# Fused chunked attention and a two-layer block: program order by a list scheduler, whole-chunk attention, ordered loads, quarter stripes

## The chip, the cores and the metric

The kernel runs on one core of one Trainium2 chip. Its engines are named as in the profiles: PE or TensorE (matmuls; PEld is its weight load), ACT or ScalarE and DVE or VectorE (element-wise work and copies), POOL or GpSimd (most casts of Q and K here, and the weight loads), SP or SyncE (issues the other loads and the stores). Matmuls write to PSUM, and a copy by ACT or DVE takes the result from there. The metric is the device time of one execution in microseconds (us). Repeated executions of one kernel mostly agree within 0.5%, a few are 1% longer. A profiled execution also has a span, from its first instruction to its last; the reported time is some 1.7 us longer than the span (265.2 against 263.5 us in the profiled run of the kernel before).

## The reference

Linear attention with a decay per head, in blocks, followed by two matrix products with a smooth activation between them (4 batches, 8 heads, 768 tokens, head dimension 64; 3072 tokens, model width 512, hidden width 2048):

```python
for b in range(nb):                                # blocks of 64 tokens
    intra = einsum('bhic,bhjc->bhij', qb, kb) * Dmask
    intra = einsum('bhij,bhjd->bhid', intra, vb)
    inter = einsum('bhid,bhde->bhie', qb * lam_pow, kv_state)
    out[:, :, sl] = intra + inter
    kv_state = lam_block * kv_state + einsum('bhsd,bhse->bhde', kb_dec, vb)
x = out.transpose(0, 2, 1, 3).reshape(3072, 512)
h = x @ w_in
g = where(h >= 1, h, where(h <= -1, 0, (h + 1) ** 2 / 4))
return g @ w_out
```

## The kernel before

Both kernels fold the decay into Q and K by tables, and work on 24 chunks of 128 tokens. Four chunks make a stripe of 512 tokens. A stripe goes through the first layer (16 blocks of 128 hidden units, four 128x512 matmuls each, into `ph`), ReLU on ACT, the rest of the activation on DVE (`t`, `w`, `gT`), and the second layer (16 groups of four 128x512 matmuls into `py`). Attention works on half chunks (four heads), and each half passes through three stages with one PSUM buffer each:

```python
def stage_t(u):     # transposes of Q, K with V and identity; copies out of PSUM
    ...             # 2 transposes into pq, 2 matmuls 128x256 into pk
    for hi in range(2):
        nc.scalar.copy(out=qb[hi*64:hi*64+64, :, hi, :], in_=pq[hi*64:hi*64+64])
    nc.scalar.copy(out=t, in_=pk[:, :, 1, :])                       # kT
    nc.vector.tensor_tensor(t, pk[:, :, 0, :], U[u - 2], op=AX.add) # running state
def stage_s(u):     # scores, 2 matmuls 128x256, then the causal mask on DVE
    ...
def stage_o(u):     # state and scores times V into po, then two copies to xT on ACT
    ...
```

The order is written by hand. Before the main loop stripe 0 is attended and chunk 4 begun; in the loop a block of the first layer of stripe `s` alternates with a step of attention for stripe `s+1` and a group of the second layer of stripe `s-1`:

```python
load_w_in(...)                       # rest of the first weights
for i in range(WS):
    load_w_out(i)                    # second weights, all at once
ensure_loaded(CPS + 1)
ensure_cast(CPS)                     # chunk 4
a, b_ = att_step()
for f in a + b_:
    f()
...
for s in range(NST + 1):
    for i in range(FO):
        ...                          # loads, casts
        if s < NST:
            l1(s, i)
        for f in todo_a:             # attention of later chunks
            f()
        if s < NST:
            smelu(s, i)
        if s > 0:
            l2(s - 1, i)             # second layer: one stripe behind
        for f in todo_b:
            f()
```

So the second layer of stripe 0 stands behind the first block of stripe 1, and that needs all four chunks of stripe 1 attended.

Of the kernel before, what the change touches and what calls it, by code (L numbers as in the profile page):

```python
# [23 lines left out]
def kernel(  # L24
# [18 lines left out]
    C = 128  # L43
# [11 lines left out]
    NU = NCH * 2  # L55
# [3 lines left out]
    ld = ctx.enter_context(tc.tile_pool(name="ld", bufs=6))  # L59
    qkp = ctx.enter_context(tc.tile_pool(name="qkp", bufs=3))  # L60
    ktp = ctx.enter_context(tc.tile_pool(name="ktp", bufs=3))
    scp = ctx.enter_context(tc.tile_pool(name="scp", bufs=2))
    up = ctx.enter_context(tc.tile_pool(name="up", bufs=3))
    xp = ctx.enter_context(tc.tile_pool(name="xp", bufs=3))
    gp = ctx.enter_context(tc.tile_pool(name="gp", bufs=2))
    rp = ctx.enter_context(tc.tile_pool(name="rp", bufs=3))
# [4 lines left out]
    pp_q = ctx.enter_context(tc.tile_pool(name="pp_q", bufs=1, space=PS))  # L71
    pp_k = ctx.enter_context(tc.tile_pool(name="pp_k", bufs=1, space=PS))
# [6 lines left out]
    qkv_ld = {}  # L79

    def load(c):
        b, s0 = c // NCB, (c % NCB) * C
        ts = []
        for name, src in (("q", q), ("k", k), ("v", v)):
            t = ld.tile([128, H, D], F32, name=f"{name}f", tag=f"{name}f")
            nc.sync.dma_start(out=t, in_=src[b, :, s0:s0 + C, :].rearrange("h p d -> p h d"))
            ts.append(t)
        qkv_ld[c] = ts

    lam_b = const.tile([128, H], F32)  # L90
    nc.sync.dma_start(out=lam_b, in_=lam.partition_broadcast(128))
    load(0)
    load(1)
# [7 lines left out]
    nc.gpsimd.iota(pos_i, pattern=[[C, NCB]], base=-S // 2, channel_multiplier=1)  # L101
    pos = const.tile([128, NCB], F32)
    nc.vector.tensor_copy(pos, pos_i)
    arg = const.tile([128, NCB, H], F32)
# [5 lines left out]
    causal = const.tile([128, 128], F32)  # L110
    nc.gpsimd.memset(causal, 1.0)
    nc.gpsimd.affine_select(
        out=causal, in_=causal, compare_op=AX.is_ge, fill=0.0,
        base=0, pattern=[[1, 128]], channel_multiplier=-1)
    one = const.tile([128, 1], F32)
    nc.vector.memset(one, 1.0)

    NQ = 3
    qbd = []
    for i in range(NQ):  # L120
        t = const.tile([128, 2, 2, 128], BF16, name=f"qbd{i}")
        nc.vector.memset(t, 0.0)
        qbd.append(t)
    NV = 3
    vi = []
    for i in range(NV):
        t = const.tile([128, HP, 2, 128], BF16, name=f"vi{i}")
        nc.vector.tensor_copy(t[:, :, 1, :], _bc(ident, 1, HP))
        vi.append(t)
# [8 lines left out]
    def load_w_in(i):  # L138
        n = d_ff // WS
        nc.gpsimd.dma_start(out=w_in_sb[:, :, i * n:(i + 1) * n], in_=w_in_r[:, :, i * n:(i + 1) * n])  # L140

    def load_w_out(i):
        n = FO // WS
        nc.gpsimd.dma_start(out=w_out_sb[:, i * n:(i + 1) * n, :], in_=w_out_r[:, i * n:(i + 1) * n, :])


    qs, ks = {}, {}

    def cast(c, k_eng):
        qf, kf, vf = qkv_ld.pop(c)  # L150
        cb = c % NCB
        t = qkp.tile([128, H, D], BF16, name="qs", tag="qs")
        nc.gpsimd.tensor_tensor(t, qf, _bc(tab_q[:, cb, :], 2, D), op=AX.mult)  # L153
        qs[c] = t
        t = qkp.tile([128, H, D], BF16, name="ks", tag="ks")
        k_eng.tensor_tensor(t, kf, _bc(tab_k[:, cb, :], 2, D), op=AX.mult)  # L156
        ks[c] = t
        nc.scalar.copy(out=vi[c % NV][:, :, 0, :], in_=vf.rearrange("p (a b) d -> p a (b d)", b=2))  # L158

    kT, U, sc_sb, xT = {}, {}, {}, {}  # L160

    def stage_t(u):
        c, hf = u // 2, u % 2
        cb = c % NCB
        pq = pp_q.tile([128, 2, 128], BF16, name="pq", tag="pq")
        pk = pp_k.tile([128, 2, 2, 128], F32, name="pk", tag="pk")
        for j in range(2):
            hp = 2 * hf + j
            nc.tensor.transpose(out=pq[:, j, :], in_=qs[c][:, 2 * hp:2 * hp + 2, :].rearrange("p a d -> p (a d)"),  # L169
                                identity=ident)  # L170
        for j in range(2):
            hp = 2 * hf + j
            nc.tensor.matmul(pk[:, j], lhsT=ks[c][:, 2 * hp:2 * hp + 2, :].rearrange("p a d -> p (a d)"),  # L173
                             rhs=vi[c % NV][:, hp], start=True, stop=True)
        qb = qbd[u % NQ]
        for hi in range(2):
            nc.scalar.copy(out=qb[hi * 64:hi * 64 + 64, :, hi, :], in_=pq[hi * 64:hi * 64 + 64])  # L177
        t = ktp.tile([128, 2, 128], BF16, name="kT", tag="kT")
        nc.scalar.copy(out=t, in_=pk[:, :, 1, :])  # L179
        kT[u] = t  # L180
        if cb < NCB - 1:
            t = up.tile([128, 2, 128], BF16, name="U", tag=f"U{hf}")
            if cb == 0:
                nc.vector.tensor_copy(t, pk[:, :, 0, :])
            else:
                nc.vector.tensor_tensor(t, pk[:, :, 0, :], U[u - 2], op=AX.add)  # L186
            U[u] = t

    def stage_s(u):
        ps = pp_s.tile([128, 4, 128], F32, name="ps", tag="ps")  # L190
        for j in range(2):
            nc.tensor.matmul(ps[:, 2 * j:2 * j + 2, :], lhsT=kT[u][:, j, :], rhs=qbd[u % NQ][:, j],  # L192
                             start=True, stop=True)
        t = scp.tile([128, 4, 128], BF16, name="sc", tag="sc")
        nc.vector.tensor_tensor(t, ps, _bc(causal, 1, 4), op=AX.mult)  # L195
        sc_sb[u] = t

    def stage_o(u):
        c, hf = u // 2, u % 2
        cb = c % NCB  # L200
        st, off = c // CPS, (c % CPS) * C
        po = pp_o.tile([128, 2, 2, 128], F32, name="po", tag="po")
        for j in range(2):
            hp = 2 * hf + j
            if cb > 0:
                nc.tensor.matmul(po[:, j], lhsT=U[u - 2][:, j, :], rhs=qbd[u % NQ][:, j], start=True, stop=False)  # L206
            nc.tensor.matmul(po[:, j], lhsT=vi[c % NV][:, hp, 0, :], rhs=sc_sb[u][:, 2 * j:2 * j + 2, :],  # L207
                             start=(cb == 0), stop=True)
        if st not in xT:
            xT[st] = xp.tile([128, KO, MS], BF16, name="xT", tag="xT")  # L210
        for hi in range(2):
            nc.scalar.copy(out=xT[st][hi * 64:hi * 64 + 64, 2 * hf:2 * hf + 2, off:off + C],  # L212
                           in_=po[hi * 64:hi * 64 + 64, :, hi, :])

    def att(i):

        u, odd = i // 2, i % 2
        a, b_ = [], []
        if not odd:
            if u < NU:  # L220
                a.append(lambda: stage_t(u))
            if 1 <= u <= NU:
                b_.append(lambda: stage_o(u - 1))
        elif u < NU:
            a.append(lambda: stage_s(u))
        return a, b_


    gT, r_t, py_t = {}, {}, {}

    def l1(s, ni):
        ph = pp_h.tile([128, MS], F32, name="ph", tag="ph")
        for ko in range(KO):
            nc.tensor.matmul(ph, lhsT=w_in_sb[:, ko, ni * 128:(ni + 1) * 128], rhs=xT[s][:, ko, :],  # L234
                             start=(ko == 0), stop=(ko == KO - 1))
        if ni % 2 == 0:
            r_t[s] = rp.tile([128, 2, MS], BF16, name="r", tag="r")
        nc.scalar.activation(out=r_t[s][:, ni % 2, :], in_=ph, func=AF.Relu, bias=one[:, 0:1])  # L238

    def smelu(s, ni):  # L240
        if ni % 2 == 0:
            return
        r = r_t[s]
        if ni == 1:
            gT[s] = gp.tile([128, FO, MS], BF16, name="gT", tag="gT")
        t = rp.tile([128, 2, MS], BF16, name="t1", tag="t1")
        nc.vector.tensor_scalar(t, r, 0.5, 1.0, op0=AX.mult, op1=AX.min)
        w = rp.tile([128, 2, MS], BF16, name="w1", tag="w1")
        nc.vector.tensor_tensor(w, r, t, op=AX.subtract)  # L249
        nc.vector.tensor_tensor(gT[s][:, ni - 1:ni + 1, :], w, t, op=AX.mult)  # L250

    def l2(s, i):
        ms, kg = i // 4, i % 4
        if kg == 0:
            py_t[s] = pp_y.tile([128, d_model], F32, name="py", tag="py")
        py = py_t[s]
        for ko in range(4 * kg, 4 * kg + 4):
            nc.tensor.matmul(py, lhsT=gT[s][:, ko, ms * 128:(ms + 1) * 128], rhs=w_out_sb[:, ko, :],  # L258
                             start=(ko == 0), stop=(ko == FO - 1))
        if kg == 3:  # L260
            o = op.tile([128, d_model], F32, name="osb", tag="osb")
            nc.scalar.copy(out=o, in_=py)  # L262
            m0 = s * MS + ms * 128
# [40 lines left out]
    for f in a + b_:  # L304
        f()
# [60 lines left out]
```

## Time and profile before

263.2 us (median; 263.1 to 264.8).

| Stretch of the span, us | TensorE busy | what is there |
|---|---|---|
| 0 to 30 | 15.3 of 30 | attention of stripe 0 |
| 30 to 40 | 0 | nothing |
| 40 to 80 | 29.0 of 40 | first layer of stripe 0, attention of stripe 1 |
| 80 to 200 | 119.3 of 120 | everything interleaved, TensorE full |

From the page of the kernel before, its second part: one digit for each fortieth of the span (6.6 us), the busy share in tenths; `PEclk` is the recorded clock of TensorE in tenths, `DMA` the busy share of the DMA engines, `GB/s` what they moved.

```profile
PE   0567306666889999999999999999999999999993
ACT  4768303778996977797779777977796754554210
PEclk9999755999999999999999999999999999999998
DMA  6999999999990526753574357110111011111122
GB/s 134 210 217 187 196 196 220 210 226 218 218 202 2 138 67 120 159 128 85 108 159 121 88 113 163 40 40 0 42 41 40 2 40 40 40 42 40 40 80 80
```

The first twelve slices (to 78 us) have the DMA full and TensorE half idle; from then on it is the other way round. The table of windows of the same kernel gives busy us of each engine in each stretch, the number of its instructions, the recorded clock, the DMA share and GB/s.

```profile
core 0: us, PE busy (x) PEld busy (x) DVE busy (x) ACT busy (x) POOL busy (x), PEclk, DMA share, GB/s
30.00:40.00 10.00, 0.00 (x0) 0.10 (x1) 0.00 (x0) 0.00 (x0) 1.04 (x1) 0.65 1.21 196
40.00:50.00 10.00, 6.85 (x27) 3.29 (x27) 1.12 (x2) 4.90 (x11) 2.69 (x3) 0.67 1.16 213
50.00:60.00 10.00, 6.89 (x43) 3.96 (x45) 8.74 (x11) 8.12 (x20) 5.83 (x6) 1.00 1.14 225
60.00:70.00 10.00, 6.78 (x45) 3.72 (x45) 8.36 (x15) 8.68 (x23) 2.59 (x2) 1.00 1.32 218
70.00:80.00 10.00, 8.50 (x53) 4.84 (x53) 8.92 (x15) 9.56 (x23) 4.64 (x4) 1.00 1.16 189
80.00:100.00 20.00, 19.89 (x118) 11.10 (x119) 12.64 (x24) 15.48 (x36) 4.08 (x4) 1.00 0.30 74
```

The waits from 20 to 80 us name the longest one (us in total, times, longest):

```profile
PE pk L173 <- ACT vi_152 L158: 12.6, 1, 12.6
ACT vi_152 L158 <- DMA vf<-in_v_dram: 11.9, 1, 11.9
```

and TensorE's timeline (start, duration, instruction, what ended the idle time before it) shows the hole it makes:

```profile
28.55 0.42 PE L169 MATMUL pq<-ident,qs 128*128 128x128 bf16 x2
41.53 0.58 PE L173 MATMUL pk<-vi_152,ks 128*128 128x256 bf16 x2 [12.56 <-ACT vi_152 L158]
```

TensorE takes its instructions in order. Chunk 4's matmuls wait for V; chunk 3's last step and the first layer of stripe 0, whose weights had landed by 31.2 us, stand behind them.

The same timeline gives the price of matmuls, from start to start. At full rate ("warm" below), two of 128 columns take 0.11 us, two of 256 take 0.22, four of 512 take 0.86 (the last from four blocks in a row elsewhere); early in the run one of 256 columns takes 0.21 to 0.22 us, half the rate:

```profile
19.68 0.42 PE L206 MATMUL po<-qbd_144,U 128*128 128x256 bf16 x1
19.90 0.42 PE L207 MATMUL po<-sc,vi_152 128*128 128x256 bf16 x1
...
120.33 0.28 PE L169 MATMUL pq<-ident,qs 128*128 128x128 bf16 x2
120.44 0.38 PE L173 MATMUL pk<-vi_152,ks 128*128 128x256 bf16 x2
120.66 1.03 PE L258 MATMUL py<-w_out_sb,gT 128*128 128x512 bf16 x4
```

### The profile page before, as it was taken

Reading aid. Unit: us, or ns where it says so; the run is one execution under the profiler, and the core shown is the slowest. Engines: PE = TensorE matmul, PEld = TensorE weight load, DVE = VectorE, ACT = ScalarE, POOL = GpSimd, SP = SyncE. Lnnn points to the kernel's source line nnn. Section 1 sums busy time; section 2 is a strip of 40 time slices with the busy share of each in tenths; the row PEclk is TensorE's granted clock in tenths of the full one; section 3 lists DMA queues with packets and bytes.
Section 4 is the critical chain, followed back from the end, with each engine's and each line's share of the span. In section 5 each row is a group of like instructions: output and inputs, shape, how many; then the busy total and the mean of one; then the engine's idle time right before and its main releaser. Section 6 shows DMA issues by size and latency. Waiting matters only on the chain.

```text
span 263.5 us, 3576 instructions
## 1 busy us (share of the span) xinstructions
PE 222.8 (85%) x1209; PEld 118.7 (45%) x1232; DVE 143.8 (55%) x245; ACT 173.7 (66%) x389; POOL 54.2 (21%) x61
## 2 busy tenths in 40 slices
PE   0567306666889999999999999999999999999993
PEld 0234203333445555555555555555555544444441
DVE  3554201388887576657574766574747645555300
ACT  4768303778996977797779777977796754554210
POOL 3418111552340332033303320333000000000000
PEclk9999755999999999999999999999999999999998
DMA  6999999999990526753574357110111011111122
GB/s 134 210 217 187 196 196 220 210 226 218 218 202 2 138 67 120 159 128 85 108 159 121 88 113 163 40 40 0 42 41 40 2 40 40 40 42 40 40 80 80
DMA packets 82721, 29.58 MB, mean 112 GB/s; under 512 B 75536, under 2 KB 79632, under 8 KB 82704
## 3 DMA queue, kind: packets, MB, share of 16 engines
q1 hardware_dynamic: 78480, 25.18, 45.5%
q0 software_dynamic: 4224, 4.19, 9.7%
q8 instruction: 9, 0.15, 0.3%
q14 instruction: 8, 0.07, 0.1%
HBM read 27.27 MB, written 6.29 MB: 127 GB/s over the span
## 4 chain that ended last, share of the span: by engine, by line
PE 69%; DVE 3%; ACT 1%; issue 0%; ACTq 0%
PE py L258 31%; PE ph L234 26%; PE po L207 3%; PE ps L192 3%; PE pk L173 2%; PE po L206 2%; PE pq L169 1%; DVE gT L250 1%; DVE w_726 L249 1%; DVE sc L195 0%; DVE w_768 L249 0%; ACT r L238 0%; DVE U L186 0%; ACT xT L212 0%; ACT osb L262 0%
## 5 line engine op out<-in xcount | busy, mean ns | idle before, releaser
L234 PE MATMUL ph<-xT,w_in_sb 128*128 128x512 bf16 x380 | 99.6, 383 | 1.7 <-ACT r L238 1.3
L238 ACT ACTIVATE r<-ph,one 128x512 bf16<-128x512 f32 x96 | 65.9, 687 | 43.3 <-PE ph L234 39.6
L258 PE MATMUL py<-w_out_sb,gT 128*128 128x512 bf16 x365 | 92.3, 379 | 1.0
L234 PEld LDWEIGHTS <-w_in_sb 128*128 128x128 bf16 x384 | 37.9, 99 | 37.6 <-issue 2.8
L258 PEld LDWEIGHTS <-gT 128*128 128x128 bf16 x384 | 37.6, 98 | 32.3
L153 POOL TENSOR_TENSOR qs<-qf,tab_q 128x512 bf16<-128x512 f32 x24 | 25.3, 1052 | 121.7 <-PE pq L169 92.0
L186 DVE TENSOR_TENSOR U<-pk,U 128x256 bf16<-128x256 f32 x32 | 13.6, 424 | 56.5 <-ACT kT L179 56.5
L212 ACT CAST xT<-po 64x256 bf16<-64x256 f32 x96 | 35.3, 367 | 4.5 <-PE po L207 3.7
L195 DVE TENSOR_TENSOR sc<-ps,causal 128x512 bf16<-128x512 f32 x48 | 32.9, 685 | 4.6 <-PE ps L192 4.0
L156 POOL TENSOR_TENSOR ks<-kf,tab_k 128x512 bf16<-128x512 f32 x20 | 22.3, 1117 | 7.9 <-DMA kf<-in_k_dram 7.9
L262 ACT COPY osb<-py 128x512 f32<-128x512 f32 x24 | 14.2, 591 | 12.4 <-PE py L258 12.4
L169 PE MATMUL pq<-ident,qs 128*128 128x128 bf16 x96 | 14.3, 235 | 6.7 <-POOL qs L153 6.7
L179 ACT CAST kT<-pk 128x256 bf16<-128x256 f32 x48 | 17.9, 372 | 2.4 <-PE pk L173 1.3
L173 PE MATMUL pk<-vi_152,ks 128*128 128x256 bf16 x32 | 6.8, 298 | 14.6 <-ACT vi_152 L158 12.6
L169 PEld LDWEIGHTS <-qs 128*128 128x128 bf16 x96 | 10.1, 106 | 16.8 <-POOL qs L153 6.7
L173 PEld LDWEIGHTS <-ks 128*128 128x128 bf16 x96 | 8.1, 103 | 20.5 <-issue 8.1
L192 PEld LDWEIGHTS <-kT 128*128 128x128 bf16 x96 | 8.5, 101 | 19.4 <-ACT kT L179 11.0
L158 ACT CAST vi_152<-vf 128x512 bf16<-128x512 f32 x8 | 4.9, 610 | 11.9 <-DMA vf<-in_v_dram 11.9
L177 ACT COPY qbd_146<-pq 64x256 bf16<-64x256 bf16 x32 | 11.6, 361 | 1.6 <-PE pq L169 1.2
L177 ACT COPY qbd_144<-pq 64x256 bf16<-64x256 bf16 x32 | 11.5, 361 | 0.6 <-PE pq L169 0.2
L177 ACT COPY qbd_148<-pq 64x256 bf16<-64x256 bf16 x32 | 11.5, 361 | 0.5
L206 PEld LDWEIGHTS <-U 128*128 128x128 bf16 x80 | 8.2, 102 | 7.8 <-issue 3.7
(187 smaller groups left out, 213.9 us busy)
## 6 DMA issues: line engine op xcount, KB each, us to landing
qf<-in_q_dram SPq DMA_DIRECT2D x24, 256.0 KB, 4.8
kf<-in_k_dram SPq DMA_DIRECT2D x24, 256.0 KB, 4.7
vf<-in_v_dram SPq DMA_DIRECT2D x24, 256.0 KB, 5.0
out_dram<-osb SPq DMA_DIRECT2D x24, 256.0 KB, 2.0
w_in_sb<-in_moe_w_in_dram POOLq DMA_DIRECT2D x4, 512.0 KB, 8.7
w_out_sb<-in_moe_w_out_dram POOLq DMA_DIRECT2D x4, 512.0 KB, 15.5
lam_b<-in_lam_dram SPq DMA_DIRECT2D x1, 4.0 KB, 2.9
```

What stands on the lines that cost most here:

```text
L153: nc.gpsimd.tensor_tensor(t, qf, _bc(tab_q[:, cb, :], 2, D), op=AX.mult)
L156: k_eng.tensor_tensor(t, kf, _bc(tab_k[:, cb, :], 2, D), op=AX.mult)
L169: nc.tensor.transpose(out=pq[:, j, :], in_=qs[c][:, 2 * hp:2 * hp + 2, :].rearrange("p a d -> p (a d)"), identity=ident)
L173: nc.tensor.matmul(pk[:, j], lhsT=ks[c][:, 2 * hp:2 * hp + 2, :].rearrange("p a d -> p (a d)"), rhs=vi[c % NV][:, hp], start=True, stop=True)
L177: nc.scalar.copy(out=qb[hi * 64:hi * 64 + 64, :, hi, :], in_=pq[hi * 64:hi * 64 + 64])
L179: nc.scalar.copy(out=t, in_=pk[:, :, 1, :])
L192: nc.tensor.matmul(ps[:, 2 * j:2 * j + 2, :], lhsT=kT[u][:, j, :], rhs=qbd[u % NQ][:, j], start=True, stop=True)
L195: nc.vector.tensor_tensor(t, ps, _bc(causal, 1, 4), op=AX.mult)
L212: nc.scalar.copy(out=xT[st][hi * 64:hi * 64 + 64, 2 * hf:2 * hf + 2, off:off + C], in_=po[hi * 64:hi * 64 + 64, :, hi, :])
L234: nc.tensor.matmul(ph, lhsT=w_in_sb[:, ko, ni * 128:(ni + 1) * 128], rhs=xT[s][:, ko, :], start=(ko == 0), stop=(ko == KO - 1))
L238: nc.scalar.activation(out=r_t[s][:, ni % 2, :], in_=ph, func=AF.Relu, bias=one[:, 0:1])
L258: nc.tensor.matmul(py, lhsT=gT[s][:, ko, ms * 128:(ms + 1) * 128], rhs=w_out_sb[:, ko, :], start=(ko == 0), stop=(ko == FO - 1))
```

## The change

Its intent is to have TensorE full from as early as possible. Four parts:

1. Every operation (load, cast, group of matmuls, copy) becomes a node with an engine, an estimated duration, the nodes that it needs (buffers that come free included) and a deadline. A list scheduler plays the graph through on estimated durations and emits the program in that order.
2. Attention works on whole chunks: all eight transposes at once, copies twice as wide, the running state kept in PSUM by accumulation instead of DVE additions, all matmuls 128 columns wide. ACT loses most of its copies; DVE takes over those of K, and those of Q from chunk 4 on.
3. Loads are ordered: K, Q, V of chunks 0 to 3, first weights, chunk 4, second weights, the rest.
4. Stripes 1 and 2 go through the first layer in quarters of 128 tokens, so that one attended chunk gives TensorE 16 blocks' worth of work, and the second layer of that quarter follows. The second layer of stripe 0 no longer waits for stripe 1.

The core of the diff (cuts marked):

```diff
+    def run_plan(free):
+        ...                                  # deadlines go backwards through the graph
+        while len(out_seq) < len(ops):
+            t, e = min((max(free[e], min(r for r, _ in lst)), e) for e, lst in ready.items() if lst)
+            r, x = min(((r, x) for r, x in ready[e] if r <= t), key=lambda p: (p[1].due, p[0]))
+            ready[e].remove((r, x))
+            free[e] = t + x.ns
+            x.t, x.end = t, t + x.ns + x.extra
+            out_seq.append((t, len(out_seq), x))
+            ...
+        for t, _, x in sorted(out_seq, key=lambda p: p[:2]):
+            x.fn()                           # emits the instructions
...
+    QS = (1, 2)
+    ...
+        if s in QS:
+            l1 = [(1, s, i, p) for p in range(CPS) for i in range(0, FO, CPS)]
+        else:
+            l1 = [(1, s, i, 0) for i in range(FO)]
...
+    order = [("c", c) for c in range(CPS)] + [("w", 0), ("c", CPS), ("w", 1)] + [("c", c) for c in range(CPS + 1, NCH)]
...
+        add(("t", c), "PE", mm(*[128] * 8), lambda c=c: f_t(c),
+            [("cast", c, 0), ("cast", c, 1), ("kb", c - 1, 0), ("kb", c - 1, 1), ("qT", c - 1)], due=od - 6000, extra=FILL)
+        add(("qT", c), e, 600 if c < CPS else 365, ...)
+        add(("x", c), "ACT", 600, lambda c=c: f_x(c), ...)
...
+            add(("g", grp), "DVE", 220 + 512 * rw * 1.25 / .96 + 240, lambda a=(s, i, n, p, grp): f_g(*a),
+                [("r", n1), ("g", grp - 1), ("l2", (s - 1) * FO - 1)])
...
-    for s in range(NST + 1):
-        for i in range(FO):
-            ...                              # the order by hand
+    run_plan({"PE": 7000, "ACT": 6500, "DVE": 6000, "POOL": 7000, "DMA": 2000})
```

## The prediction

> **What bounds the kernel now.** From 78 us on, TensorE: the table of windows has PE 99.4% busy from 80 to 240 us, and the timeline shows matmuls back to back until 259.46 us; then 4 us of last eviction and store. Before 78 us TensorE waits: PE is busy 15 of the first 30 us, 0 of 30 to 40, 13.7 of 40 to 60, 15.3 of 60 to 80. The waits view: 12.6 us (28.6 to 41.5) behind the V cast of chunk 4, whose load came late behind weights; waits on copies of K; ACT 90% busy from 60 to 80. Matmuls ran at half rate (256 columns every 0.21 us instead of 0.11) from 6.7 to 22.8 us and from 26 to 46.6. The slices show DMA near 210 GB/s up to 78 us.
>
> **What the change does.** Warm spacing in the timeline is 0.216 us for 512 columns, 0.110 for 256, 0.055 for 128. TensorE before: 768 x 0.216 + 368 x 0.110 + 96 x 0.055 = 211 us. After, by the program text: attention 736 matmuls of 128 columns (40.9 us against 45.8), the first layer of stripes 1 and 2 as 512 of 128 columns instead of 128 of 512, four groups split 384+128: 208 us. So only 3 us of work goes. ACT loses query copies (34.6 us), K copies (17.9) and half-width xT copies (35.3 to some 14), and gains U copies: 174 to about 120 us. DVE stays near 145.
>
> The gain is the head. K, Q, V of chunks 0 to 3 load first, then first weights, chunk 4, second weights, the rest. 256 KB takes about 1.22 us at 215 GB/s, a weight quarter about 3 us (9.7% of 263 us over 8). So chunk 3 is in at 18 us, stripe 0 attended at 23, first weights complete near 30, second near 46, chunk 5 near 50. Between 23 and 46 us TensorE has 13.9 us of first layer, 1.7 of attention, 3.6 of chunk 4's quarter, 5 of second layer: just enough. Afterwards a chunk costs 3.7 us of DMA against 8.6 of TensorE.
>
> **Sum.** Dense start 23 + (207.7 - 6.3 done by then) + 2.5 for half-rate matmuls at first (before: 5 us at half rate from 41.5) + 3 for gaps up to 50 us + 4 tail = **234 us, range 229 to 243**. Chances: faster by over 2% 0.96, within 2% 0.03, slower 0.01. The saving, 29 us, is all on the critical path: the dense part begins 55 us earlier but must do most of what the old head had done.
>
> **What would show it.** Windows: PE nearly full from 25 us, over 98% after 50; the chain almost all PE. 128-column spacing 55 ns. No V-cast wait over 3 us. ACT busy 115 to 125 us. Tail 4 us.
>
> **What would make it wrong.** The Trainium skill, "TensorE: Matmul & The Clock Gate", section Back-to-back issue gap, puts a stream of weight load plus 128-column matmul at about 81 ns each. Here pairs of transposes run at 55, but no long runs exist; at 81, 1264 such matmuls would add 33 us and the gain would vanish. Second: a fixed order from estimated durations leaves engines waiting where reality differs, above all from 23 to 50 us, where a long wait would bring the half rate back. Third: if ACT's order delays evictions of the two-buffered first-layer PSUM, 50 ns per group would cost 5 us.

## The result, and the profile after

236.7 us (median of 4; 236.5 to 237.7) against 263.2 us. The ratio is 0.898, with a 95% interval of 0.894 to 0.903. Ratios here are the mean time of one kernel's fast runs over that of the other's in the same rounds, so not quite the ratio of the medians quoted.

The same lines of the page after (slices of 5.9 us):

```profile
PE   0487997999997999999999999999999999999993
ACT  3456566243577766666566366566455354544110
PEclk9999999999999999999999999999999999999999
DMA  6999969986999999899993011011011011110212
GB/s 139 220 212 200 192 112 185 196 162 186 247 201 218 227 221 206 191 243 228 230 255 81 19 45 37 12 45 47 0 45 47 0 45 47 45 43 2 92 51 83
```

The hole is gone, ACT has air, and the loads now run in the shade of TensorE, spread up to 123 us. The table of windows of the changed kernel, with the same columns:

```profile
30.00:40.00 10.00, 8.62 (x47) 4.07 (x47) 9.68 (x15) 7.49 (x13) 5.62 (x6) 1.00 0.85 139
40.00:50.00 10.00, 9.30 (x95) 6.36 (x96) 7.65 (x14) 2.65 (x4) 2.04 (x2) 1.00 1.11 209
50.00:60.00 10.00, 9.95 (x79) 5.75 (x78) 8.22 (x13) 4.17 (x7) 2.58 (x3) 1.00 0.67 166
60.00:70.00 10.00, 9.95 (x169) 9.52 (x168) 6.53 (x11) 7.26 (x14) 5.36 (x6) 1.00 1.16 222
70.00:80.00 10.00, 8.72 (x139) 7.89 (x138) 9.74 (x18) 7.06 (x14) 5.47 (x5) 1.00 1.00 212
80.00:100.00 20.00, 19.63 (x266) 16.17 (x268) 18.99 (x34) 13.61 (x27) 11.42 (x10) 1.00 1.04 210
```

TensorE is busy 86 to 99.5% in each row from 30 us on, where before it had 0 to 85% up to 80 us. TensorE's timeline of the changed kernel shows the start of the dense part, the longest wait left, and the quarters at work (32 matmuls of 128 columns, from 46.28 to 48.06 us, are 55.6 ns each):

```profile
22.68 0.81 PE L288 MATMUL ph<-xT,w_in_sb 128*128 128x384 bf16 x4 [0.56 <-ACT xT L275]
...
40.37 0.38 PE L252 MATMUL ps<-qT,kbd_121 128*128 128x128 bf16 x4 [1.69 <-DVE qT L236]
...
46.28 1.95 PE L295 MATMUL ph<-xT,w_in_sb 128*128 128x128 bf16 x32
48.06 1.03 PE L323 MATMUL py<-w_out_sb,gT 128*128 128x512 bf16 x3
```

(One record of the last group is missing, as a few per cent of matmul records are.)

Where did the 26.5 us come from? Not from earlier attention. I read from the traces when the last xT copy of chunk 7 ends, that is, when stripe 1 is fully attended, and summed the TensorE work of all recorded matmuls that started before that moment, at the warm spacings of above:

| kernel | stripe 0 attended, us | stripe 1 attended, us | TensorE work done by then, us: attention + first layer + second layer |
|---|---|---|---|
| before | 43.8 | 76.5 | 15.5 + 13.2 + 0 = 28.7 |
| after | 26.3 | 73.3 | 14.3 + 24.1 + 12.3 = 50.7 |

The copies that end these stretches, in the kernel before and after (start, duration):

```profile
75.78 0.74 ACT L212 CAST xT<-po 64x256 bf16<-64x256 f32 x2
72.73 0.58 ACT L275 CAST xT<-po 128x512 bf16<-128x512 f32 x1 [0.17 <-PE po L268]
```

Stripe 1 is attended only 3.2 us earlier. But by then TensorE has done 22.0 us more, nearly all of the second layer of stripe 0 and three quarters of stripe 1. With the 3 us by which the whole work is shorter (208 against 211 us, by the prediction's sum) that is 28.2 us, and the two profiled spans differ by 28.7 (263.5 and 234.8; the profiled run of before was 2 us slower than its median). The old kernel could do none of this work, because its order put it behind the complete stripe 1.

### The profile page after: what moved, and what is told of

It reads as the page before. It is cut to its first block, busy times and chain, and to the rows that moved or that the text cites. A ratio compares the mean times of both kernels' runs of the same rounds, so it can differ in the third digit from the quotient of the medians.

```text
span 234.8 us, 4665 instructions
## 1 busy us (share of the span) xinstructions
PE 213.8 (91%) x1876; PEld 137.1 (58%) x1904; DVE 160.3 (68%) x274; ACT 123.4 (53%) x216; POOL 59.4 (25%) x64
## 4 chain that ended last, share of the span: by engine, by line
PE 75%; DVE 16%; ACT 3%; DMA 2%; issue 2%; SPq 0%; ACTq 0%
PE py L323 33%; PE ph L295 26%; PE ps L252 5%; DVE gT L315 4%; PE pt L229 4%; PE po L268 4%; DMA x2f<-in_v_dram 2%; DVE sc L258 2%; PE pu L242 2%; PE po L265 2%; ACT r L303 1%; DVE kbd_121 L232 1%; PE ph L288 1%; DVE kbd_120 L232 1%; DVE qT L236 1%
## 5 line engine op out<-in xcount | busy, mean ns | idle before, releaser
L295 PE MATMUL ph<-xT,w_in_sb 128*128 128x128 bf16 (+1 forms) x744 | 93.1, 269 | 1.0 <-ACT r L303 0.4
L295 PEld LDWEIGHTS <-w_in_sb 128*128 128x128 bf16 x752 | 53.0, 98 | 28.0 <-issue 1.4
L219 POOL TENSOR_TENSOR ks<-x1f,tab_k 128x512 bf16<-128x512 f32 x21 | 24.0, 1141 | 93.0 <-DMA x1f<-in_k_dram 38.9
L219 POOL TENSOR_TENSOR qs<-x0f,tab_q 128x512 bf16<-128x512 f32 x23 | 25.8, 1123 | 7.0 <-DMA x0f<-in_q_dram 6.9
L275 ACT CAST xT<-po 128x512 bf16<-128x512 f32 x24 | 14.0, 585 | 11.9 <-PE po L268 11.8
L229 PE MATMUL pt<-ident,ks 128*128 128x128 bf16 x96 | 10.1, 232 | 0.1
L229 PE MATMUL pt<-ident,qs 128*128 128x128 bf16 x96 | 10.0, 231 | 0.0
L252 PE MATMUL ps<-qT,kbd_121 128*128 128x128 bf16 x64 | 6.8, 229 | 3.0 <-DVE qT L236 1.7
L236 DVE COPY qT<-pt 128x512 bf16<-128x512 bf16 x20 | 8.5, 425 | 0.3
L252 PEld LDWEIGHTS <-kbd_121 128*128 128x128 bf16 x64 | 4.9, 102 | 5.8 <-DVE kbd_121 L232 2.6
L252 PE MATMUL ps<-qT,kbd_120 128*128 128x128 bf16 x64 | 6.8, 229 | 1.4 <-ACT qT L236 1.1
L252 PE MATMUL ps<-qT,kbd_122 128*128 128x128 bf16 x64 | 6.5, 225 | 1.3 <-DVE qT L236 0.8
L252 PEld LDWEIGHTS <-kbd_120 128*128 128x128 bf16 x64 | 4.8, 102 | 3.8 <-DVE kbd_120 L232 1.8
```

Source lines behind the costliest of these rows:

```text
L219: eng.tensor_tensor(t, qkv_ld[c, x], _bc(tab[:, c % NCB, :], 2, D), op=AX.mult)
L229: nc.tensor.transpose(out=ptt[c][:, i, hp, :], in_=pair(x[c], hp), identity=ident)
L236: (nc.scalar.copy if e == "ACT" else nc.vector.tensor_copy)(qT[c], ptt[c][:, 0])
L252: nc.tensor.matmul(pst[c, g][:, 2 * j + hi, :], lhsT=kbd[c % NKB][:, 2 * g + j, hi, :], rhs=qT[c][:, 2 * g + j, :], start=True, stop=True)
L275: nc.scalar.copy(out=xT[sx][:, :, off:off + C], in_=pot[c])
L295: nc.tensor.matmul(ph[:, j * m:(j + 1) * m], lhsT=w_in_sb[:, ko, (ni + j) * 128:(ni + j + 1) * 128], rhs=xT[s][:, ko, part * m:(part + 1) ...
```

## The experiments

Twelve kernels ran; all gave correct results.

| run | edit | median, us | ratio to before (95%) |
|---|---|---|---|
| (the change) | | 236.7 | 0.898 (0.894 to 0.903) |
| e1 | before: first layer ahead of chunk 4 | 267.0 | 1.011 (1.001 to 1.020) |
| e2 | before: second weights behind chunk 4 | 264.1 | 0.999 (0.991 to 1.007) |
| e12 | before: both | 267.3 | 1.012 (1.004 to 1.020) |
| e3 | after: no quarters | 244.9 | 0.925 (0.918 to 0.931) |
| e3b | after: quarters in stripe 1 alone | 237.3 | 0.900 (0.896 to 0.904) |
| e4 | after: second weights ahead of chunk 4 | 239.8 | 0.908 (0.905 to 0.911) |
| e5 | after: order by deadline, no timed plan | 259.1 | 0.981 (0.975 to 0.986) |
| e6 | after: ACT's old load given back | 245.7 | 0.931 (0.928 to 0.934) |
| e7 | after: TensorE warmed up | 235.9 | 0.894 (0.891 to 0.898) |
| e8 | after: nine durations of the plan mended | 235.1 | 0.892 (0.888 to 0.896) |
| e9 | after: stores on ACT's queue | 239.3 | 0.907 (0.903 to 0.911) |
| e10 | after: e7 and e8 | 234.5 | 0.888 (0.885 to 0.892) |

### The old kernel, mended by hand: e1, e2, e12

My theory was the hole at 28.6 us: something stood in line ahead of work that was ready. If so, small edits of the old kernel should win a good part of the gain. The rival was the load of attention on ACT and DVE.

e1 leaves chunk 4's casts and attention out until eight blocks of the first layer are issued, and presses the remaining steps into the other eight:

```diff
-    ensure_cast(CPS)
-    a, b_ = att_step()
-    for f in a + b_:
+    HOLD = 8
+    held, b_ = att_step()
+    for f in b_:
         f()
...
+            if g == HOLD:
+                ensure_cast(CPS)
+                todo_a += held
```

> The kernel before, with one thing moved: the first eight blocks of stripe 0's first layer stand ahead of chunk 4's casts and attention in every engine's order, instead of behind them; loads unchanged. In the trace of before, TensorE stood from 28.6 to 41.5 us at chunk 4's attention although the first weights had landed at 18.1, 22.7, 27.8 and 31.2 us and stripe 0 was attended at about 29 us. Theory 1 (the gain of the change is the head: what stands in line ahead of what): 7 us of first layer run inside that hole, so 263.2 becomes 252 to 257. Theory 2 (the gain is the lighter attention, which unloads ACT and DVE in the stage from 43 to 78 us): moving a block that ACT and DVE will have to catch up with later buys under 3 us, 260 to 263.

e2 moves the loop `for i in range(WS): load_w_out(i)` behind `ensure_cast(CPS)`.

> The kernel before, with the second layer's weight loads issued after chunk 4's casts instead of before them, as in the changed kernel. Chunk 4's V landed at 40.8 us because 4.2 MB of second-layer weights shared the DMA with it. Theory 1: V lands near 34 us, all that follows moves up by 5 to 7 us, 256 to 259. Theory 2 (attention's weight on ACT and DVE): under 3 us, 260 to 263, because the stage after it takes as long as ACT needs.

e12 does both.

> The kernel before with both edits, the first layer's first eight blocks ahead of chunk 4 and the second weights behind it. Theory 1: the two overlap, because both fill the same hole, but the stage from 43 to 78 us also has less to do and starts earlier: 247 to 254, that is, half of the whole gain without touching attention. Theory 2: 258 or more. If it comes near 240, attention by whole chunks and the timed plan bought almost nothing.

Measured: 267.0, 264.1 and 267.3 us. Theory 1 as I had stated it falls: e1 and e12 are even slower, by 1%, at the edge of what these runs resolve, and e1 and e2 lie above the ranges of both theories. The edits did what they were to do. In e2 chunk 4's V landed at 31.4 us instead of 40.8; in e1 and e12 stripe 0 was attended at 29.6 and 31.4 us instead of 43.8, and the first layer ran at once. (The expectation of e1 has stripe 0 attended at about 29 us in the kernel before; that was wrong, its last step stood in the hole too.) Yet stripe 1 was attended at 77.2 (e1), 74.4 (e2) and 79.7 us (e12), against 76.5, and in each of the three TensorE had done the same 28.7 to 28.9 us of work by then. The hole only moved. In e1 and e2 one can see where to. ACT takes its instructions in order too, and the cast of a later chunk's V stands on it ahead of copies that TensorE needs. In e1 it stood 6.0 us for chunk 5's V and TensorE 7.8 us behind that; in e2 the wait for chunk 4's V shrank from 12.6 to 4.5 us, and a new one opened at chunk 6's V:

```profile
50.10 0.62 ACT L158 CAST vi<-vf 128x512 bf16<-128x512 f32 x1 [10.19 <-DMA vf<-in_v_dram]
52.40 0.61 PE L192 MATMUL ps<-qbd,kT 128*128 128x256 bf16 x2 [9.59 <-ACT kT L179]
```

So these two runs do not show what an old kernel without such waits would do. e12 is the cleaner one: TensorE waits 0.2 us for chunk 4's V, and none of its later waits up to 80 us is longer than 3.8. The windows of e12:

```profile
50.00:60.00 10.00, 4.90 (x22) 2.57 (x23) 4.94 (x6) 7.58 (x18) 4.34 (x4) 0.64 1.20 219
60.00:70.00 10.00, 6.55 (x35) 3.58 (x35) 5.08 (x10) 6.17 (x15) 2.04 (x2) 0.84 1.37 218
70.00:80.00 10.00, 6.81 (x31) 3.56 (x29) 5.30 (x8) 6.54 (x16) 4.70 (x4) 0.50 0.94 153
```

TensorE, DVE and ACT are all far from full there, so the rival in its plain form, ACT's load, does not hold either: with half of the blocks gone, the half chunks follow each other one chain at a time (transposes, copies, scores, mask), and little fills the waits (0.9 to 2.0 us each for the copies of K from 58 to 77 us). The low clock (0.50 to 0.84) makes the matmuls that remain dearer. What the four old orders share is that the work within TensorE's reach before stripe 1 is attended is about 29 us, however it is shuffled, and that stripe 1 was not attended before 74 to 80 us in any of them.

### Quarters: e3, e3b

e3 is the changed kernel with `QS = ()`, e3b with `QS = (1,)`.

> The changed kernel without quarters: stripes 1 and 2 of the first layer in 128x512 blocks, which need all four chunks of a stripe. Theory 1 (TensorE is fed by one chunk at a time while loads are scarce): chunk 7 is loaded at about 63 us and attended near 67, until when TensorE has only stripe 0 and attention, 35 us of work from 22.7 us on, so some 8 us of idle time appear between 55 and 68 us, less 1 us for cheaper matmuls: 241 to 246. Rival: quarters are cosmetic, because attention of the chunks is ready in time, 235 to 238.

> The changed kernel with quarters in stripe 1 alone. Without any quarters it took 244.9. If it is only the scarcity of loads up to about 60 us that makes quarters pay, stripe 2 needs none, and its 256 narrow matmuls are 0.5 us dearer: 235.5 to 237.5. If attention's pace up to 100 us is what quarters hide, stripe 2 without them costs 2 to 5 us: 238.5 to 242.

Without quarters 244.9 us, 8.2 us lost, as the first theory said. It is the table of above once more: in e3 stripe 1 is attended even earlier, at 67.6 us, but TensorE has done only 41.1 us of work by then, no stripe 1 among it. Counted as elapsed time less work done, e3 is 5 us behind the changed kernel by 70 us (the expectation had some 8); it loses another 4 us between 80 and 120 us, where stripe 2 comes in whole blocks too. With quarters in stripe 1 alone it is 237.3 us, not to be told from 236.7. So stripe 1's quarters are the 8 us; stripe 2's buy nothing that these runs resolve.

### Load order: e4

```diff
-    order = ... [("w", 0), ("c", CPS), ("w", 1)] + ...
+    order = ... [("w", 0), ("w", 1), ("c", CPS)] + ...
```

(with the needs of these loads adapted)

> The changed kernel with one part undone: the second layer's weights load before chunk 4's K, Q and V instead of behind them; the plan knows of it. Three edits of the kernel before showed that load order alone gives it nothing (264.1) and that moving the first layer ahead of chunk 4 costs it 4 us. Theory A (load order is a main part of the gain): chunk 4 lands near 46 us, its quarter comes near 51 us, and TensorE, which has 27.8 us of stripe 0 to do from 22.7 us on and can start its second layer earlier, waits little: but attention of chunks 4 to 7 is pressed together afterwards; 241 to 247. Theory B (with quarters and a plan any order that keeps the DMA busy serves): 235 to 240.

239.8 us, 3.1 us lost: the value lies in theory B's interval, at its upper end. Chunk 4 is attended at 54.9 us instead of 46.2, TensorE's idle time from 30 to 60 us even shrinks, from 2.5 to 0.5 us, since the second layer of stripe 0 has its weights early; but from 60 to 100 us it grows from 2.0 to 7.2 us. The order of loads is worth 3 us under a plan, and nothing in the old kernel (e2).

### The timed plan: e5

The same graph, deadlines and resources; but the program is emitted from a heap of operations whose inputs are emitted, the earliest deadline first, with no clock.

```diff
-        while len(out_seq) < len(ops):
-            t, e = min(...)
-            ...
+        while ready:
+            _, _, x = heapq.heappop(ready)
+            x.fn()
+            for u in users[x.key]:
+                left[u.key] -= 1
+                if left[u.key] == 0:
+                    n += 1
+                    heapq.heappush(ready, (u.due, n, u))
```

> The changed kernel without the timed plan: same graph, same deadlines, same loads, but the program order is simply by deadline among operations whose inputs stand earlier in the program; no durations decide when an engine takes what. Theory P (the timed plan is what keeps the engines from waiting in line): gaps of 0.5 to 2 us at many attention steps up to 100 us, 245 to 256. Rival (deadlines and whole-chunk attention are enough; the plan's clock adds little): 236 to 241.

259.1 us: 22.4 of the 26.5 us are gone, more than I had expected at most. Its waits over the whole span:

```profile
ACT r L295 <- DVE w L305: 52.0, 22, 3.7
PE ps L244 <- DVE sc L250: 12.8, 14, 4.4
```

The second line is the plainest: the two halves of a chunk's scores use one PSUM buffer, and in this order they often stand next to each other, so TensorE waits for the mask on DVE between them. In the timeline one such wait is 4.4 us (at 18 us), and from 105 to 182 us one of some 0.6 us stays for nearly every chunk, long after the head, where the planned order puts other matmuls between and TensorE is full. Stripe 0 is attended at 32.5 us instead of 26.3. So whole-chunk attention, quarters and load order do not bring the gain by themselves; the order of the instructions must suit them. This is one other order, though, and no bound: an order by hand might be much better than this one.

### ACT's load: e6

```diff
-        (nc.scalar.copy if e == "ACT" else nc.vector.tensor_copy)(qT[c], ptt[c][:, 0])
+        for hi in range(2):
+            for g in range(2):
+                nc.scalar.copy(out=qT[c][HD[hi], 2*g:2*g+2], in_=ptt[c][HD[hi], 0, 2*g:2*g+2])
```

and the same for xT; the plan is told 1440 and 1470 ns.

> The changed kernel with ACT's old load given back: the transposed Q of every chunk leaves PSUM on ACT in four pieces of 64 partitions x 2 head pairs, and so does xT, as in the kernel before; ACT busy should rise from 123 to about 173 us, as before, and DVE lose 8; the plan is told the new durations. Rival R (the old kernel was held by ACT's load in its head, and lifting it is the gain): the time goes back by 8 us or more, above 244. Theory C (ACT's load is not the limit, since in the edited old kernel TensorE idled while ACT was 62 to 72% busy; what held it was one half-chunk chain at a time in fixed order): 237 to 242, from a longer chain per chunk at the start alone.

ACT's busy time rose to 166.5 us and the time to 245.7 us, 9.0 us more. By what I had written down, that speaks for rival R: lighter attention on ACT is worth having. Stripe 1 was attended at 81.2 us instead of 73.3. But the edit raises two things at once, ACT's load and the length of each chunk's chain (by some 0.9 us at each of the two copies, by the plan's figures), and the plan made another order of it. That the load itself, and not the chain, costs the 9 us is not shown.

### What is left: e7, e8, e9, e10

From 22.7 us on, TensorE's start-to-start times in the changed kernel leave 5.9 us of idle time: 3.6 us up to 50 us, 1.7 us from 71 to 76 us, and 0.6 us later (the 5.7 us in the expectation of e8 are the gaps over 0.15 us). The largest piece is the wait that ends at 40.37 us, 1.85 us from start to start, for a copy on DVE. DVE and POOL at that time:

```profile
30.51 1.41 POOL L219 TENSOR_TENSOR ks<-x1f,tab_k 128x512 bf16<-128x512 f32 x1 [11.64 <-DMA x1f<-in_k_dram]
32.70 1.06 POOL L219 TENSOR_TENSOR qs<-x0f,tab_q 128x512 bf16<-128x512 f32 x1
...
31.06 1.42 DVE L315 TENSOR_TENSOR gT<-w_444,t_442 128x1024 bf16<-128x1024 bf16 x1
32.39 1.66 DVE L311 TENSOR_SCALAR t_464<-r 128x1024 bf16<-128x1024 bf16 x1
...
39.01 0.87 DVE L232 COPY kbd_121<-pt 64x512 bf16<-64x512 bf16 x2
39.89 0.42 DVE L236 COPY qT<-pt 128x512 bf16<-128x512 bf16 x1
```

Elsewhere the same two DVE instructions take 0.69 and 0.42 us. Here they end 0.6 and 0.3 us after POOL's casts, which end at 31.92 and 33.76 us. The Trainium skill offers a reason in "SBUF — State Buffer", section SBUF: two separate sides: Vector and GpSimd share a port pair, and "The shared pair is an exclusive lock, not a bandwidth split". The trace fits that: the two are 0.73 and 1.24 us longer, as if held until the cast was done. So does the whole trace: of the 144 activation instructions on DVE, 113 overlap no cast on POOL and none of these is over 0.43 us (`t`) or 0.70 us (`w`, `gT`); 19 are longer, and each of them overlaps a cast. It is no proof: no run changed POOL's casts alone, and by the recorded starts the second of the two DVE instructions began before its cast (32.39 against 32.70 us), so which came first cannot be read here. The plan does not know it. DVE is 2 us behind the plan by 35 us, and the copies that chunk 4's scores need stand behind two groups of activation that the plan had thought done.

e8 tells the plan, and changes no operation:

```diff
-  220 + 512 * rw * 1.25 / .96 + 240
+  220 + 512 * rw * 1.25 / .96 + 240 + (700 if grp in (1, 2, 8, 9, 10, 11, 12, 17, 18) else 0)
```

> The changed kernel with nine durations of its plan mended: groups 1, 2, 8 to 12, 17 and 18 of the activation arithmetic on DVE took 0.4 to 1.24 us more than planned, when POOL cast K and Q at the same time; the plan is told 0.7 us more for these. No operation changes, only the order made of them. If the 5.7 us of TensorE's idle time after 22.7 us (largest: 1.85 us at 38.5, where chunk 4's scores stand behind groups that ran late, and 1.7 us at 71 to 76) come from the plan's wrong durations, half of it goes: 233.5 to 235.5. If the plan is tight as it is, 236.2 to 238.

235.1 us. The wait at 38 us shrinks from 1.85 to 1.1 us and those from 71 to 76 us to 0.3; idle time after 30 us falls from 4.9 to 2.8 us. The two intervals against before (0.888 to 0.896, 0.894 to 0.903) overlap a little, so that the 1.6 us is likely rather than certain, though all six runs (234.2 to 236.2 us) are faster than all four of the change (236.5 to 237.7), taken in other rounds; the trace shows where it comes from.

e7 puts 54 matmuls of the identity, never read, at the start:

```diff
+    warm = pp_u.tile([128, HP, 128], F32, name="pu", tag="pu")
+    for i in range(54):
+        nc.tensor.matmul(warm[:, i % HP, :], lhsT=ident, rhs=ident, start=True, stop=True)
```

> The changed kernel with 54 idle 128-column matmuls of the identity ahead of the first real one, from about 1.5 to 7 us, when TensorE has nothing else to do. In its trace the matmuls of the first chunks ran at half rate (107 ns for 128 columns) from 7.67 to 19 us, 80 of them, 4.1 us more than at full rate. If the head hangs on TensorE's own pace, the first layer starts at 21 us instead of 22.7 and the time falls by 1 to 2 us, 234.7 to 235.7. If it hangs on arrivals of K, Q, V (chunk 3 landed at 17.6 us) and on copies, matmuls run at 56 ns and the time stays within 0.5 us of 236.7.

235.9 us, with the first layer starting at 21.5 instead of 22.7 us. The gain of 0.8 us is between the two expectations and the intervals overlap. Its timeline of TensorE tells why it is not more:

```profile
1.43 5.45 PE L94 MATMUL pu<-ident 128*128 128x128 bf16 x54 [1.43 <-POOL ident masks.py:199]
7.65 0.38 PE L245 MATMUL pu<-vi,ks 128*128 128x128 bf16 x4 [0.77 <-ACT vi L226]
...
10.60 0.64 PE L232 MATMUL pt<-ident,ks 128*128 128x128 bf16 x4
14.27 0.39 PE L232 MATMUL pt<-ident,ks 128*128 128x128 bf16 x4
```

Four matmuls span 0.38 us at 7.65 us, full rate, but 0.64 us at 10.60: the rate has halved again, after 3 us (7 to 10 us) in which TensorE was busy for 0.99, and it comes back at 13.0 us, from where matmuls of 128 columns start 55 ns apart.

e9 sends the stores through ACT's queue (`nc.scalar.dma_start`, 400 ns more for each in the plan), because SyncE's queue, in order too, stood from 48.3 to 53.25 us at the first store while loads waited behind it.

> The changed kernel with its output stores issued from ACT's queue instead of SyncE's, so that loads never stand behind a store: in its trace SyncE's queue stood from 48.3 to 53.25 us at the first store, and chunk 6's V landed at 58.6 instead of some 53 us. If those 5 us were on the chain, DVE has chunk 6's work before its crowded stretch from 64 to 77 us and the time falls by 1 to 2 us: 234.7 to 235.7. If loads have slack by then, it stays within 0.5 us of 236.7, or rises a little because ACT issues 24 stores.

Chunk 6's V landed at 53.3 us instead of 58.6, and the time rose to 239.3 us. Earlier loads alone did not help. Why it is slower is open: ACT issues more, but the plan also made another order of the longer durations, with new waits of 1.9 us at 61 and 1.8 us at 85 us.

e10 joins e7 and e8.

> The changed kernel with both edits that helped: 54 idle matmuls at the start and the nine mended durations. Apart they gave 0.8 and 1.6 us, by medians of their runs against 236.7. If they act on different stretches (the head up to 22 us; the waits from 38 to 76 us), they add: 233.7 to 235.0. If the shifted head puts the plan out of step again, 235 to 237.

234.5 us, ratio 0.888 (0.885 to 0.892), clear of the change's own 0.894 to 0.903: the fastest version here.

## Why the prediction was right

**The time.** 234 predicted, 236.7 measured, within the range of 229 to 243. The sum was one of spans, and the span came out at 234.8; the 1.7 us by which a reported time exceeds the span was left out. That is most of the miss.

**Loads and dense start.** Predicted: chunk 3 in at 18 us, first weights near 30, second near 46, chunk 5 near 50, dense start at 23. The trace: 17.6, 29.1, 46.5, 49.6 and 22.7. Transfer times taken from the old trace carried over, because the DMA was full in both.

**TensorE's work.** 128-column matmuls were the main risk. They run at 55.6 to 56 ns in rows of 32 with a new weight load for each, where the Trainium skill's 81 ns ("TensorE: Matmul & The Clock Gate", Back-to-back issue gap) would have cost 33 us, by the prediction's estimate. Pairs in the old trace were a good enough sample.

**Half rate and gaps.** Two mis-sized terms that cancelled, by luck. 2.5 us for matmuls at half rate in the dense part: none, since the full rate was there from 19 us on, before that part began. 3 us of gaps up to 50 us: 3.6 us there, but 2.3 us later, 5.9 in all. "Over 98% after 50" was wrong for 70 to 80 us, where TensorE was 87% busy and DVE 97%. The sign "the chain almost all PE" did not show either: the page after gives PE 75% and DVE 16% of the chain (before: 69% and 3%).

**DVE.** "Stays near 145" was wrong: 160.3 us. The step that failed is the count of copies: the prediction took copies of Q and K off ACT and did not put them on DVE. There they take 28.6 us, while what DVE no longer does (state additions, copies into `vi`) was 17.7. Set-up at the start adds some 3.6 us. Waiting for POOL's casts counts as busy, but the kernel before had it as well: some 8.6 us over the normal durations before, 10.2 after, so it explains less than 2 of the 16.5 us. Such waits do lie ahead of the largest gap; the prediction named wrong durations of the plan as a risk, and e8 shows that this risk came true at a size of 1 to 2 us. **ACT** at 123.4 us and the tail (last matmul begins at 230.4, span ends at 234.8 us) were as predicted.

**The cause.** Here the prediction was weaker than its number. It named the wait of 12.6 us for chunk 4's V first among the limits. e1 and e12 took it from ahead of the first layer, e2 shortened it to 4.5 us, and the old kernel did not gain, though in e1 and e2 new waits of 7.8 and 9.6 us opened. Its other statement, that the dense part begins 55 us earlier but must do most of what the old head had done, is what the counts bear out: 50.7 against 28.7 us of TensorE work when stripe 1 is attended, although attention itself is only 3 us earlier. Quarters (8.2 us, e3), the planned order (22.4 us against plain deadlines, e5), lighter copies on ACT (9.0 us, e6) and load order (3.1 us, e4) each cost time when undone; they overlap, and do not add up to 26.5. Only part of that is the count above. When stripe 1 is attended, elapsed time less work done is 47.8 us in the kernel before, 22.6 in the changed one, 26.5 in e3, 27.5 in e6 and some 31 in e5, but 21.6 in e4: all that e4 loses, and more than half of what e5 loses, comes later. One direct test was not made: the old kernel with only the second layer of stripe 0 moved ahead of stripe 1. How much of the gain that alone would bring is open.

## What to carry to other kernels

When an engine idles in a head that waits for loads, count the work that its program order lets it reach before the next barrier; removing the longest wait gained nothing here, where that sum stayed the same and the wait moved to the next load. A finer unit of hand-over (a quarter of a stripe) and letting the next layer start on finished parts raise the sum. A static order from estimated durations was worth 22 us here against one plain deadline order, but it is only as good as these durations: measure them where engines run together, and mend the ones that are off. And when work leaves one engine, add it to the sum of the engine that takes it.

## What the Trainium skill lacked or had wrong

- "TensorE: Matmul & The Clock Gate", Back-to-back issue gap: it gives about 81 ns per matmul for streams of weight load and 128-column matmul and about 131 ns at 512 columns in real kernels. Here it is 55.6 to 56 ns and 216 ns, which is what its formula for isolated matmuls says; the "sustained" figures fit nothing in these traces.
- The same page, Part 1 and the table under "Why this matters for your kernels": a return to the half rate is told as following an idle window of about 3.4 us, and gaps over about 3 us are to be avoided. In e7 the rate halved by 10.6 us although the timeline shows no idle gap after 6.9 us longer than 1.35 us; TensorE was busy 0.99 of the 3 us from 7 to 10 us. Low use without a long gap was enough. The page's section on a second HAM failure mode does tell of such a return through frequent short idle times, but gives no figure for how little use suffices.
- The same page warns that clock records can be unreliable. In the kernel before they agree with the spacing of matmuls wherever there is a record (half rate from 26.1 to 29.5 and from 32.9 to 46.6 us). But the first record lies at 22.7 us, and before it the profile's views print 1.00, while 256 columns take 0.21 to 0.22 us instead of 0.11: at the beginning of a trace, start-to-start times show the rate.
- "SBUF — State Buffer" describes a port lock between Vector and GpSimd that fits these traces. What it does not say is how it looks in a profile: the waiting is inside the busy time (0.42 becomes 1.66 us, 0.69 becomes 1.42), some 10 of DVE's 160.3 us in the changed kernel.
